# Mirrored spectral pairs, deeper weight prefetch and new filler rates in a fused forward and backward block

## The chip, the cores and the metric

The kernel runs on one core of one Trainium2 chip. The metric is device time in microseconds (us), the median of several executions. "PE" is TensorE, "PEld" its weight load, "DVE" VectorE, "ACT" ScalarE, "POOL" GpSimd, "SP" SyncE.

## The reference

The reference computes one block and all gradients of it. An adaptive layer norm goes into a spectral filter (a two-dimensional real Fourier transform, a complex product with a filter, and back), a second layer norm goes into a bilinear gated layer, and then everything is differentiated.

```python
# x: (1, 2048, 576) bf16; w_r, w_i: (2048, 289); w_gate, w_up: (576, 4608); w_down: (4608, 576)
def _A_ref(x, w_r, w_i):
    X = jnp.fft.rfft2(x.astype(jnp.float32), axes=(-2, -1))
    X = X * (w_r + 1j * w_i)
    return jnp.fft.irfft2(X, s=(S, D), axes=(-2, -1)).astype(jnp.bfloat16)
def _B_ref(x, w_gate, w_up, w_down):
    h = (x @ w_gate) * (x @ w_up)
    return h @ w_down
# sa, ca, ga, sb, cb, gb: six rows of silu(c) @ w_mod
h = layernorm(x) * (1 + ca) + sa
x = x + ga * _A_ref(h, w_r, w_i)
h = layernorm(x) * (1 + cb) + sb
x = x + gb * _B_ref(h, w_gate, w_up, w_down)
# outputs: x and, by jax.vjp with grad_out, the gradients of x, w_r, w_i, w_gate, w_up, w_down, c, w_mod
```

## The kernel before

The transforms are matrix products. The 2048 points are split as 16 times 128, and the spectral part works on eight pairs of the 16 residues k2: (0, 8) and (k, 16 − k). For each pair, `pz` is the transform along D, `px` the one along the 128 points, `cA` the product with the filter, and `pb` the way back. This happens twice: in the head (forward) and in the tail (backward, with the gradient of the filter in `g_w`).

The program has these stages, and the text uses these names for them: the start (loads, transposes, first transforms), the head pairs, the head's way out (`pv`, `py`), the rest of `ghp`, the main loop (the gated layer, about 980 us), t1 (first half of the tail), the tail pairs, t4 (the tail's way out with layer norm gradient), the close (remaining filler) and the end.

TensorE is kept busy by filler: the spectral stages are generators, and at each `yield r` the driver lets r units of independent products run. In the head the filler is `ghp` (the gradient through w_down); in the tail it is `po` (the forward output product, one unit is 18 matmuls).

```python
def pair_x(st, i, kk, gt, fps, ev):                  # 8 matmuls for each kk, 16 for a pair
    C, Sn, nC, nS = (gt[:, kk, v, :] for v in range(4))
    # ... i == 0 cut
    if kk == 0:
        terms = [[(C, 0, 0), (Sn, 0, 1), (Sn, 1, 0), (nC, 1, 1)], [(nS, 0, 0), (C, 0, 1), (C, 1, 0), (Sn, 1, 1)]]
    else:
        terms = [[(C, 0, 0), (Sn, 0, 1), (nS, 1, 0), (C, 1, 1)], [(nS, 0, 0), (C, 0, 1), (nC, 1, 0), (nS, 1, 1)]]
    # ... each c: four matmuls accumulate into px[:, c]; ScalarE evicts px to X (bf16)

def pairs(...):                                       # the order for one pair, `fill` = units of filler
    for i in range(8):
        yield fill
        z(i + 2, 0)
        yield fill
        z(i + 2, 1)
        x(i + 1, 0)
        yield fill
        x(i + 1, 1)                                   # evicts X, then cmul on VectorE makes Ys[i + 1]
        pair_b(i, 0, Ys[i], tbb[i], ut, fps, ev)
        yield fill
        pair_b(i, 1, Ys[i], tbb[i], ut, fps, "a")
        on_b(i, st[i]["X"])                           # tail: g_w, the gradient of the filter

# head:  fill 0.5;  filler ghp, its weights loaded AH blocks ahead
AH = 4
def ghh_units():
    for fb, k in ...:
        if k == 0 and fb + AH < NFB:
            load_wdT(fb + AH)                         # two transposing DMAs
        st = u4w.tile([128, 8, 128], BF, name="ghh_st", bufs=4)
        # ... 10 matmuls into pg (ghp), ScalarE evicts pg to st, DMA writes st to DRAM

# tail pairs: fill 0.35;  t4: 1.55 units at each of 16 steps;  then the close runs what is left
yield from pairs(wk, gsp, T, hT, ut, fps, True, lambda i, X: None, g_w, 0.35, "a")
# g_w: pA, pB are f32 products of the saved spectrum and the gradient; gw = their sum and difference (bf16)
```

## Time and profile before

| | before |
|---|---|
| median of the 4 runs known at the prediction | 1561.51 us (1551.31 to 1568.61) |
| span of the profiled execution | 1566.8 us |
| PE busy | 1502.3 us, 96% |
| DVE busy | 805.6 us, 51% |
| main loop's first matmul | 272.56 us |

The page of the kernel before starts with the busy time of each engine, its share of the span, and its number of instructions.

```profile
PE 1502.3 (96%) x11275; PEld 1035.4 (66%) x11275; DVE 805.6 (51%) x1867; ACT 486.9 (31%) x827; POOL 307.3 (20%) x514
```

TensorE is the bound: a page with 96% there leaves 64 us of idle time in all. The view of waits for PE says where that idle time went. The columns are: the waiting engine, tile and line, what it waited for, the total in us, how many times, and the longest.

```profile
PE gwp L607 <- DMA hh_sf<-hhT: 10.0, 5, 2.8
PE py L329 <- DVE dm L815: 7.2, 2, 6.7
PE ghp L440 <- DMA wdT<-in_B_w_down_dram: 6.7, 1, 6.7
PE po L944 <- DMA wdr<-in_B_w_down_dram: 4.7, 2, 3.8
PE gwp L607 <- DVE so L611: 4.0, 1, 4.0
...
PE ghp L440 <- ACT ghh_st L441: 3.7, 3, 1.6
```

Several of these are single waits of 4 to 7 us, and two of them (wdT and wdr) are late loads of weights, which a program can simply issue earlier.

The table of stretches gives the busy time of each engine in a window. The columns are the window, its length, busy us with the number of instructions in brackets for PE, PEld, DVE, ACT and POOL, the granted TensorE clock as a share of full speed, the busy share of the DMA engines, and GB/s.

```profile
75.00:160.00 85.00, 84.56 (x566) 54.84 (x565) 27.41 (x41) 39.36 (x55) 22.62 (x45) 1.00 0.60 171
258.00:265.40 7.40, 0.75 (x4) 0.14 (x3) 0.00 (x0) 1.01 (x1) 1.06 (x2) 0.92 0.50 125
265.40:272.50 7.10, 7.10 (x20) 2.56 (x20) 0.00 (x0) 1.01 (x1) 0.54 (x1) 0.61 0.29 60
1352.00:1427.00 75.00, 72.52 (x596) 57.73 (x594) 52.93 (x83) 35.26 (x55) 18.92 (x37) 1.00 0.75 241
```

The first and last rows are the two spectral stages: PE is busy nearly all of both, so matmuls removed there are worth their time, if nothing else takes their place. The two rows between are the wait for wdT and what follows it. The second is nearly empty, and in the third the granted clock is 0.61. The timeline of PE around that place (start, duration, engine, line, operation, in brackets the idle time ahead and what ended it) shows the cost:

```profile
249.96 8.79 PE L440 MATMUL ghp<-goT,wdT 128*128 128x512 bf16 x40 [0.62 <-ACT ghh_st L441]
265.40 7.23 PE L440 MATMUL ghp<-goT,wdT 128*128 128x512 bf16 x20 [6.65 <-DMA wdT<-in_B_w_down_dram]
272.56 0.60 PE L656 MATMUL abp<-h2T,wgu 64*128 64x512 bf16 x4
```

Forty matmuls took 8.79 us before the gap, and the next twenty took 7.23 us, where half of 8.79 would be 4.4.

The view by tile counts the matmuls of the spectral part (operation, output and inputs, number; then shortest, median and longest duration in ns, and the first and last start):

```profile
L226 PE MATMUL px<-zt,gt x240: 283/287/288, 75.0 to 1418.4; 128*128 128x290 bf16 x120
...
L243 PE MATMUL pb<-gbt,cA x360: 270/273/283, 85.2 to 1427.1; 128*128 128x256 bf16 x180
```

The 287 ns are the latency of one; pipelined, they follow each other every 0.11 to 0.125 us.

### The profile page before, as it was taken

Reading aid. Unit: us, or ns where it says so; the run is one execution under the profiler, and the core shown is the slowest. Engines: PE = TensorE matmul, PEld = TensorE weight load, DVE = VectorE, ACT = ScalarE, POOL = GpSimd, SP = SyncE. Lnnn points to the kernel's source line nnn. Section 1 sums busy time; section 2 is a strip of 40 time slices with the busy share of each in tenths; the row PEclk is TensorE's granted clock in tenths of the full one; section 3 lists DMA queues with packets and bytes.
Section 4 is the critical chain, followed back from the end, with each engine's and each line's share of the span. In section 5 each row is a group of like instructions: output and inputs, shape, how many; then the busy total and the mean of one; then the engine's idle time right before and its main releaser. Section 6 shows DMA issues by size and latency. Waiting matters only on the chain. (4 is left out here: it accounts for less than half of the span.)

```text
span 1566.8 us, 28323 instructions
## 1 busy us (share of the span) xinstructions
PE 1502.3 (96%) x11275; PEld 1035.4 (66%) x11275; DVE 805.6 (51%) x1867; ACT 486.9 (31%) x827; POOL 307.3 (20%) x514
## 2 busy tenths in 40 slices
PE   7899998999999999999999999999999988999788
PEld 4466553568667767766856866776676666777566
DVE  5533572624633653553462464365356377467664
ACT  4554553230231132123023023112212334444323
POOL 2132343212211211111111121121120121122210
PEclk9999999999999999999999999999999998999899
DMA  9965797957865874895595686587467497667663
GB/s 283 210 185 169 223 250 212 154 116 136 157 118 123 161 160 91 142 169 118 134 142 105 145 159 144 96 157 170 96 150 144 89 323 256 218 193 261 211 227 95
DMA packets 408993, 262.12 MB, mean 167 GB/s; under 512 B 322555, under 2 KB 374012, under 8 KB 408604
## 3 DMA queue, kind: packets, MB, share of 16 engines
q1 hardware_dynamic: 374810, 143.61, 44.8%
q0 software_dynamic: 34048, 116.70, 27.1%
q8 instruction: 88, 1.44, 0.4%
q14 instruction: 45, 0.37, 0.1%
q10 hardware_dynamic: 2, 0.00, 0.0%
HBM read 107.30 MB, written 77.15 MB: 118 GB/s over the span
## 5 line engine op out<-in xcount | busy, mean ns | idle before, releaser
L688 PE MATMUL abp<-wT,ggT 128*128 128x288 bf16 x1152 | 283.0, 286 | 0.0
L689 PE MATMUL abp<-wT,guT 128*128 128x288 bf16 x1152 | 283.0, 286 | 0.0
L662 PE MATMUL abp<-h2T,wgu 128*128 128x512 bf16 x1152 | 261.1, 380 | 0.0
L694 DVE TENSOR_TENSOR acc<-acc,abp 128x288 f32<-128x288 f32 x544 | 240.8, 453 | 20.5 <-PE abp L689 5.3
L668 DVE TENSOR_TENSOR guT<-ghh,gT 128x512 bf16<-128x512 bf16 x144 | 61.3, 425 | 360.1 <-ACT gT L664 355.8
L620 PEld LDWEIGHTS <-h2p 128*128 128x128 bf16 x2304 | 225.7, 98 | 30.4 <-issue 3.4
L621 ACT CAST wo<-gwp 128x256 bf16<-128x256 f32 x144 | 53.5, 372 | 600.4 <-PE gwp L620 567.0
L662 PEld LDWEIGHTS <-wgu 128*128 128x128 bf16 x1152 | 106.8, 98 | 149.5 <-issue 30.5
L440 PE MATMUL ghp<-goT,wdT 128*128 128x512 bf16 x720 | 165.5, 384 | 11.2 <-DMA wdT<-in_B_w_down_dram 6.7
L607 PE MATMUL gwp<-gon,hh_sf 128*128 128x288 bf16 x1152 | 149.4, 291 | 14.0 <-DMA hh_sf<-hhT 10.0
L944 PE MATMUL po<-wdr,hl 128*128 128x288 bf16 x1152 | 153.4, 292 | 4.7 <-DMA wdr<-in_B_w_down_dram 4.7
L607 PEld LDWEIGHTS <-hh_sf 128*128 128x128 bf16 x1152 | 114.0, 99 | 46.3 <-DMA hh_sf<-hhT 11.6
L944 PEld LDWEIGHTS <-hl 128*128 128x128 bf16 x1152 | 114.0, 100 | 38.4 <-issue 7.7
L688 PEld LDWEIGHTS <-ggT 128*128 128x128 bf16 x1152 | 112.7, 98 | 30.2
L689 PEld LDWEIGHTS <-guT 128*128 128x128 bf16 x1152 | 112.7, 98 | 30.0
L620 PE MATMUL gwp<-gu_sf,h2p 128*128 128x256 bf16 x1152 | 130.1, 274 | 2.0 <-ACT wo L621 2.0
L440 PEld LDWEIGHTS <-wdT 128*128 128x128 bf16 x720 | 70.7, 99 | 91.1 <-issue 9.1
L620 PE MATMUL gwp<-gg_sf,h2p 128*128 128x256 bf16 x1152 | 129.3, 273 | 0.0
L612 POOL TENSOR_TENSOR dgb_p<-dgb_p,pr 128x288 f32<-128x288 f32 x72 | 58.0, 805 | 295.4 <-DVE pr L610 290.4
L664 ACT CAST gT<-abp 128x512 bf16<-128x512 f32 x144 | 84.4, 586 | 84.0 <-PE abp L662 84.0
L441 ACT CAST ghh_st<-ghp 128x1024 bf16<-128x1024 f32 x72 | 72.5, 1009 | 94.6 <-PE ghp L440 61.5
L664 ACT CAST uT<-abp 128x512 bf16<-128x512 f32 x144 | 84.4, 586 | 46.1 <-PE abp L662 46.1
(181 smaller groups left out, 1530.9 us busy)
## 6 DMA issues: line engine op xcount, KB each, us to landing
ghhT_d<-ghh_st POOLq DMA_DIRECT2D x72, 256.0 KB, 4.0
ghh<-ghhT_d POOLq DMA_DIRECT2D x36, 512.0 KB, 8.8
hhT_d<-hhT POOLq DMA_DIRECT2D x36, 512.0 KB, 6.4
hl<-hhT_d SPq DMA_DIRECT2D x32, 576.0 KB, 8.3
out_dram<-wo SPq DMA_DIRECT2D x36, 256.0 KB, 2.4
so<-in_B_w_down_dram POOLq DMA_DIRECT2D x36, 144.0 KB, 2.4
out_dram<-so SPq DMA_DIRECT2D x36, 144.0 KB, 1.9
gbt<-tab_GB POOLq DMA_DIRECT2D x16, 320.0 KB, 4.2
```

The costliest lines, as they stand in the source:

```text
L440: nc.tensor.matmul(pg[:, b, :], lhsT=wdT[:, m, :], rhs=goT[:, ts_, m, :], start=(m == 0), stop=(m == 4))
L441: nc.scalar.copy(st[:], pg[:].rearrange("f b (t p) -> f (b t) p", p=128))
L607: nc.tensor.matmul(pw[:, 0:288], lhsT=hh_sf[:, j, t, :], rhs=gon[:, t, h * 288:(h + 1) * 288], start=(t == 0), stop=(t == NT - 1))
L612: nc.gpsimd.tensor_tensor(out=dgb_p[:, hs_], in0=dgb_p[:, hs_], in1=pr[:], op=ADD)
L620: nc.tensor.matmul(pw[:], lhsT=h2p[:, t, m * 128:(m + 1) * 128], rhs=sf[:, :, t, :], start=(t == 0), stop=(t == NT - 1))
L662: nc.tensor.matmul(pts[k][i][:], lhsT=wgu[:, 4 * i + m, cs], rhs=h2T[:, ts_, m, :], start=False, stop=(m == 3))
L664: nc.scalar.copy(dst[:], pts[k][i][:])
L668: nc.vector.tensor_tensor(out=guT[:, ts_, :], in0=ghh[:, ts_, :], in1=gu[0][:], op=MUL)
L688: nc.tensor.matmul(pu[:, 0:288], lhsT=ggTs[j][:, t, :], rhs=wT[:, 0, j, hs_], start=(j == 0), stop=False)
L689: nc.tensor.matmul(pu[:, 0:288], lhsT=guTs[j][:, t, :], rhs=wT[:, 1, j, hs_], start=False, stop=(j == G - 1))
L694: nc.vector.tensor_tensor(out=dst, in0=dst, in1=pu[:, 0:288], op=ADD)
L944: nc.tensor.matmul(po[:, 0:288], lhsT=hl[:, fb, j * 128:(j + 1) * 128], rhs=wdr[fb][0][:, fb - wdr[fb][1], hs_], start=(fb == 0), stop=(fb ...
```

## The change

The intent is to use a symmetry. The rows of residue 16 − k are those of residue k in mirrored order, so one cosine and one sine product serve both members of a pair. VectorE then forms the sum and the difference of the even part E and the odd part O. This halves `px` and `pb` for seven of eight pairs, in head and tail. The second member comes out with its rows k1 reversed, so the filter is first copied in DRAM in mirrored order (`wrev_d`), and the gradient is written mirrored (`grev_d`) and copied back. Around it, other things move:

- wdT is loaded nine blocks ahead instead of four, and `ghh_st` has five buffers instead of four.
- In the tail the leftover rows of the last weight gradient go first, the first `po` products are split in another order, and one load of wdr is issued one step later.
- The row `rc` is loaded ahead.
- The filler rates go from 0.35 to 0.5 in the tail pairs and from 1.55 to 1.4 in t4.
- Some pools have other depths, and one memset goes from POOL to VectorE.

The core of the diff, with cuts marked:

```diff
-            for v, m in enumerate((C, Sn, -C, -Sn)):
+            for v, m in enumerate((C, Sn, -Sn)):
                 G[:, i, kk, v, :] = m
...
         elif kk == 0:
-            terms = [[(C, 0, 0), (Sn, 0, 1), (Sn, 1, 0), (nC, 1, 1)], [(nS, 0, 0), (C, 0, 1), (C, 1, 0), (Sn, 1, 1)]]
+            terms = [[(C, 0, c), (Sn, 1, c)] for c in (0, 1)]
         else:
-            terms = [[(C, 0, 0), (Sn, 0, 1), (nS, 1, 0), (C, 1, 1)], [(nS, 0, 0), (C, 0, 1), (nC, 1, 0), (nS, 1, 1)]]
+            terms = [[(C, 1, c), (nS, 0, c)] for c in (1, 0)]
...
-        evac(X[:, kk, :, :], px[:, :, 0:FQ], ev)
+        if i > 0:
+            st[i][kk] = wk.tile([128, 2, FQ], FP32, name="EO", tag="w")
+            evac(st[i][kk][:], px[:, :, 0:FQ], ev)
...
+            nc.vector.tensor_tensor(out=X4[:, 2:0:-1, :], in0=E[:], in1=O[:], op=ADD)
+            nc.vector.tensor_tensor(out=X4[:, 0:4:3, :], in0=E[:], in1=O[:], op=SUB)
... (pair_b: two terms instead of four for each half)
@@ cmul
-        return A
+        if not mix:
+            return A
+        nc.vector.tensor_tensor(out=B[:, 0, :, :], in0=A[:, 0, :, :], in1=A[:, 1, :, :], op=ADD)
+        nc.vector.tensor_tensor(out=B[:, 1, :, :], in0=A[:, 0, :, :], in1=A[:, 1, :, :], op=SUB)
+        return B
@@ head
-        AH = 4
+        AH = 9
-            wdTs[fb] = u4w.tile([128, 5, 128], BF, name="wdT")
+            wdTs[fb] = u4w.tile([128, 5, 128], BF, name="wdT", bufs=10)
-        load_wdT(3)
+        for fb in range(3, 9):
+            load_wdT(fb)
-                st = u4w.tile([128, 8, 128], BF, name="ghh_st", bufs=4)
+                st = u4w.tile([128, 8, 128], BF, name="ghh_st", bufs=5)
+                    for k, v in enumerate((wr_v, wi_v)):
+                        nc.gpsimd.dma_start(wrev_d[k], mirrored(v))
@@ tail
-        last_grads = grads(NFB - G, hh_sf, gg_sf, gu_sf)
+        last_grads = grads(NFB - G, hh_sf, gg_sf, gu_sf, True)      # left_rows first
-            nc.gpsimd.memset(h[:, :, D:D + 2], 0.0)
+            nc.vector.memset(h[:, :, D:D + 2], 0.0)
-                yield from pairs(wk, gsp, T, hT, ut, fps, True, lambda i, X: None, g_w, 0.35, "a")
+                yield from pairs(wk, gsp, T, hT, ut, fps, True, lambda i, X: None, g_w, 0.5, "a")
+            load_rc(0)
-                        yield 1.55
+                        yield 1.4
-                if k in (3, 7, 12):
+                if k in (3, 8, 12):
-                    for h in range(2):
+                    for h, k in ((0, 0), (1, 0), (0, 1), (1, 1)) if t == 0 else ((0, 0), (0, 1), (1, 0), (1, 1)):
... (mirrored writes of the gradient, table loads, pool depths: cut)
```

## The prediction

> **What bounds the kernel now.** TensorE. The page gives PE 1502 of 1567 us (96%), DVE 51%, ACT 31%. By the table of stretches PE is also busy 24–25 of every 25 us in both spectral stages that the change rewrites: 75–160 us (head pairs) and 1352–1428 us (tail pairs). PE time removed there should mostly be span. The Trainium skill, "TensorE: Matmul & The Clock Gate" (HAM oscillation), warns against PE gaps above about 3.4 us; this trace agrees: after the 6.65 us gap at 258.7 us the granted clock is 0.61 and 20 matmuls of 512 take 7.2 us instead of 4.4.
>
> **Removed.** The waits by tile give 240 matmuls for px and 360 for pb. With even/odd sums formed on VectorE, each of 7 pairs in each of two stages needs 8 instead of 16 px and 12 instead of 24 pb matmuls: 112 and 168 fewer. The timeline shows 8 px in 1.00 us and 24 pb in 2.62 us, so 0.125 and 0.109 us each: 14.0 + 18.3 = 32 us of PE, half in the head, half in the tail.
>
> **Added.** Per pair, two f32 combinations (0.756 us each for 580 elements, as the gw group) and two bf16 mixes (0.455 us): 2.4 us of DVE. Head pairs: period 10.55 us now, 8.3 after by PE; DVE about 6. Fits, but px groups are now 0.5 us, shorter than their 0.64 us ACT evictions in two PSUM buffers behind a 1.01 us ghh_st eviction: I estimate 0.7 us of new PE stall per pair. Tail pairs: DVE rises from about 6.5 to 9 us per pair, PE falls to 8.2 (with more filler), so VectorE becomes co-critical; perhaps 6 us is lost. The mirrored DRAM copy (1 MB at about 45 us, where the DMA share is already 1.0) risks a few us.
>
> **Moved.** Nine-deep wdT prefetch should remove the 6.65 us wait for wdT plus the 2.8 us of slow clock behind it. A fifth ghh_st buffer: part of 3.1 us. left_rows moved first and the split order at t = 0 take the 4.7 us wait of po on wdr. Filler rates 0.5 and 1.4 leave 10 instead of 13 po units to cover the closing chain, which exposes about 5 us. The t4 stage loses 16 us of PE to DMA and DVE waits now and will not give its whole saving.
>
> **Sum.** Head: 16 − 5 stalls + 9.4 + 2 = −22 us. Tail: 16 − 6 − 4 (t4) − 5 (end) + 4.7 + 1 = −7 to −12. In all −29 to −34: **1529 us**, 8 in 10 between 1511 and 1546. Chances: faster by over 2% 0.56, within 2% 0.42, slower 0.02.
>
> **What would show each step right.** px 128 and pb 192 matmuls; PE busy down about 30 us; head pairs' period near 9 us with short PE waits on ACT evictions of pz/px; the main loop's first matmul at about 248–252 us instead of 272.6; no wait of ghp on wdT over 2 us and no clock dip before the main loop; no wait of po on wdr; DVE over 85% busy in the tail pairs, with PE waits there on DVE.
>
> **What would make it wrong.** VectorE order: if the ut cast queues behind the new mixes, pb's PSUM is held and head pairs keep their 10.5 us. If mirrored copies starve the head, the 25–75 us stretch grows. If tail DVE backlog stretches t4, the tail gains nothing and the result is about 1540. If DVE keeps up and t4 loses its stalls, about 1512.

## The result and the profile after

| | before | after |
|---|---|---|
| median | 1555.57 us (1546.23 to 1568.61, 16 runs) | 1509.48 us (1506.74 to 1515.5, 11 runs) |
| PE busy in the profiled execution | 1502.3 us | 1460.6 us |
| DVE busy | 805.6 us | 834.9 us |
| main loop's first matmul | 272.56 us | 251.32 us |

The ratio is 0.9704, with a 95% interval from 0.9677 to 0.9731: about 3% faster. A ratio here and below is the mean time of one kernel's fast runs over that of the other's of the same rounds, so not quite the ratio of the medians that are quoted. The predicted 1529 us was too high, and the time lies just below the range that began at 1511. (The record lists a twelfth execution of after, of 1504.36 us, which its summary of 11 runs leaves out.)

The page of the kernel after, the engines:

```profile
PE 1460.6 (97%) x10995; PEld 1005.0 (67%) x10995; DVE 834.9 (55%) x1925; ACT 485.8 (32%) x827; POOL 311.0 (21%) x516
```

The waits of PE, after:

```profile
PE pb L255 <- DVE cB L334: 7.1, 3, 3.5
PE po L985 <- ACT mo L988: 5.2, 1, 5.2
PE pgc L1010 <- DVE gcf L1008: 4.9, 1, 4.9
PE px L227 <- ACT zt L158: 3.9, 12, 0.4
```

None of the five leading waits of before is among them. In their place stand the new ones: `pb` waits for the mixed product `cB` of VectorE, `px` for the evictions of ScalarE, and the last small transpose `pgc` is now exposed at the end.

The timeline of PE, after, at the place where wdT had been late:

```profile
239.79 11.60 PE L464 MATMUL ghp<-goT,wdT 128*128 128x512 bf16 x53
251.32 0.60 PE L692 MATMUL abp<-h2T,wgu 64*128 64x512 bf16 x4
```

Fifty-three matmuls in 11.60 us is 0.219 us for each, with no gap. By tile, after:

```profile
L227 PE MATMUL px<-zt,gt x128: 283/285/288, 71.0 to 1373.9; 128*128 128x290 bf16 x128
...
L255 PE MATMUL pb<-gbt,cB x168: 269/272/421, 92.5 to 1389.6; 128*128 128x256 bf16 x168
L255 PE MATMUL pb<-gbt,cA x24: 269/272/273, 80.8 to 1327.5; 128*128 128x256 bf16 x24
```

That is 128 `px` and 168 + 24 = 192 `pb`, as the prediction had them.

To see where the time came from, both kernels were profiled again (the runs b_again and a_again below), because the first profile of before had caught the slowest of its 16 runs. The boundaries of the stages are first and last matmuls of `pz`, `pv`, `abp` and `po` in the traces, and each stage is the difference of two such times.

| stage (us) | before, first profile | before, second | after, second | second after − second before |
|---|---|---|---|---|
| start | 72.6 | 71.5 | 68.5 | −3.0 |
| head pairs | 89.6 | 89.7 | 77.9 | −11.8 |
| head's way out | 64.3 | 64.3 | 64.2 | −0.1 |
| rest of ghp | 46.1 | 46.4 | 35.7 | −10.7 |
| main loop | 993.8 | 984.2 | 981.4 | −2.8 |
| t1 | 86.8 | 85.6 | 80.6 | −5.0 |
| tail pairs | 74.4 | 74.0 | 77.2 | +3.2 |
| t4 | 92.8 | 88.7 | 77.1 | −11.6 |
| close | 42.0 | 42.0 | 34.1 | −7.9 |
| end | 4.4 | 4.4 | 10.6 | +6.2 |
| span | 1566.8 | 1550.8 | 1507.3 | −43.5 |

The last four stages belong together, because the filler moves between them: they take 209.1 us before and 199.0 us after, so the tail behind t1 gained 10.1 us.

### The profile page after: what moved, and what is told of

Same layout as the page of the kernel before. It is cut to its first block, busy times and chain, and to the rows that moved or that the text cites. A ratio compares the mean times of both kernels' runs of the same rounds, so it can differ in the third digit from the quotient of the medians.

```text
span 1511.1 us, 27920 instructions
## 1 busy us (share of the span) xinstructions
PE 1460.6 (97%) x10995; PEld 1005.0 (67%) x10995; DVE 834.9 (55%) x1925; ACT 485.8 (32%) x827; POOL 311.0 (21%) x516
## 5 line engine op out<-in xcount | busy, mean ns | idle before, releaser
L646 PE MATMUL gwp<-gon,hh_sf 128*128 128x288 bf16 x1152 | 144.1, 286 | 0.0
L700 ACT CAST uT<-abp 128x512 bf16<-128x512 f32 x144 | 84.4, 586 | 46.1 <-PE abp L698 46.1
L465 ACT CAST ghh_st<-ghp 128x1024 bf16<-128x1024 f32 x72 | 72.6, 1010 | 82.2 <-PE ghp L464 62.3
```

The lines of the kernel that those rows point to most:

```text
L465: nc.scalar.copy(st[:], pg[:].rearrange("f b (t p) -> f (b t) p", p=128))
L646: nc.tensor.matmul(pw[:, 0:288], lhsT=hh_sf[:, j, t, :], rhs=gon[:, t, h * 288:(h + 1) * 288], start=(t == 0), stop=(t == NT - 1))
L700: nc.scalar.copy(dst[:], pts[k][i][:])
```

## The experiments

The kernels of one session ran on the same chip and share the runs of the kernel before; five sessions were run. Sessions 2 and 3 ran on one chip, with seven runs of before in common. A trace is one execution; the medians are of several. All kernels gave correct results.

| run | median us (range) | ratio to before | 95% interval |
|---|---|---|---|
| session 1, before | 1560.13 (1553.45 to 1566.79) | | |
| b_again | 1552.65 (one run) | | |
| b_wdt | 1545.01 (1542.82 to 1546.87) | 0.9897 | 0.9856 to 0.9938 |
| a_nowdt | 1528.53 (1523.9 to 1532.08) | 0.9794 | 0.9755 to 0.9834 |
| b_spec | 1534.71 (1531.46 to 1541.59) | 0.9841 | 0.9798 to 0.9885 |
| session 2, before | 1562.22 (1552.62 to 1569.86) | | |
| a_again | 1508.16 (1506.87 to 1516.13) | 0.9662 | 0.9611 to 0.9712 |
| a_fill | 1513.77 (1510.43 to 1518.33) | 0.9686 | 0.9628 to 0.9743 |
| a_norc | 1508.36 (1504.55 to 1514.55) | 0.9656 | 0.9605 to 0.9707 |
| a_last | 1511.71 (1508.49 to 1511.75) | 0.9669 | 0.9624 to 0.9713 |
| session 3, before | 1563.07 (1552.62 to 1569.86) | | |
| a_t4slow | 1510.79 (1509.46 to 1511.18) | 0.9666 | 0.9613 to 0.9718 |
| a_bfw | 1510.07 (1508.31 to 1511.01) | 0.9662 | 0.9617 to 0.9706 |
| a_t4fast | 1508.54 (1507.86 to 1518.01) | 0.9667 | 0.9615 to 0.9719 |
| a_latew | 1508.14 (1507.23 to 1509.65) | 0.9654 | 0.9602 to 0.9706 |
| session 4, before | 1560.72 (1552.92 to 1563.09) | | |
| a_gap | 1524.04 (1519.56 to 1524.61) | 0.9768 | 0.9736 to 0.9801 |
| a_nowdt2 | 1520.56 (1519.4 to 1523.17) | 0.9756 | 0.9719 to 0.9793 |
| a_fillbf | 1503.55 (1501.97 to 1506.92) | 0.9646 | 0.9614 to 0.9678 |
| a_both | 1509.31 (1507.18 to 1511.86) | 0.9681 | 0.9648 to 0.9713 |
| session 5, before | 1557.83 (1552.85 to 1562.3) | | |
| a_fillbf2 | 1505.68 (1501.15 to 1511.95) | 0.9669 | 0.9645 to 0.9693 |
| a_again2 | 1510.68 (1506.7 to 1516.46) | 0.9695 | 0.9673 to 0.9717 |

### The two kernels again: b_again, a_again, a_again2

No edit; each is the kernel before or after, word for word.

> The kernel before, unchanged, for a second profile. Theory 1: the 10 us that TensorE waited for hh_sf transposes in the main loop of the first profile (which was the slowest of 16 runs) are partly chance; this profile shows the first main-loop matmul at 271 to 274 us again, but under 6 us of hh_sf waits, and a span of 1548 to 1560. Rival: the waits belong to the program's order, and 9 to 11 us come back at the same places.

> The kernel after, unchanged, for a second profile. Theory: the main loop's waits on hh_sf transposes are rarer in the kernel after; main loop (first to last of its matmul groups) 979 to 983 us and under 3 us of hh_sf waits, against 984 and 994 us with 3.9 and 10.0 us in the two profiles of before. Rival: the first profile of after was lucky, and this one shows 4 us or more of such waits.

> The kernel after verbatim, beside the bf16 version on the same chip: 1505 to 1511 us, no waits on hh_sf in the first 60 us of the main loop, head pairs 77.9 us, tail pairs with t4, closing stage and end 199 us.

The span of b_again was 1550.8 us, 16.0 us less than the first profile of the same kernel. The stage table above shows where: 9.6 us in the main loop, where the first profile had waited 10.0 us for hh_sf, and 4.1 us in t4. So waits on hh_sf and in t4 come and go between executions of before; the pair b_again and a_again compares a quick execution of before with an ordinary one of after.

a_again took 1507.3 us and a_again2 1514.7 us. Nearly all of that difference is in the head pairs: 77.9 against 84.5 us (82.7 in the first profile of after). The expectation of 77.9 us for a_again2 was a miss. The waits of VectorE in a_again2 between 69 and 110 us name what had happened:

```profile
DVE cB L329 <- DMA wn<-wrev_d: 4.0, 1, 4.0
DVE cA L328 <- DMA wn<-wrev_d: 3.3, 1, 3.3
```

and its table of stretches shows the consequence for PE:

```profile
90.00:95.00 5.00, 0.51 (x5) 0.18 (x2) 2.23 (x5) 0.88 (x2) 1.04 (x3) 0.98 0.91 208
95.00:100.00 5.00, 5.00 (x22) 2.56 (x22) 4.54 (x8) 0.16 (x1) 0.69 (x2) 0.67 1.06 313
```

The mirrored filter came too late, PE stood still for 4.5 us, and the clock fell to 0.67 afterwards. In the first profile of after VectorE waited 4.2 and 1.2 us on `wrev_d` there. In a_again it did not at all. No other wait of PE between 60 and 150 us differs by more than 0.3 us, though why the copy is late in some executions was not tested. In the seventeen profiles with mirrored copies the head pairs took 77.8 or 77.9 us in thirteen, and 78.8 to 84.5 us in the other four (b_spec, a_fillbf, the first profile of after, a_again2). So the mirrored copies did hurt the head now and then, as the prediction feared, but through a late operand in the pairs and not by stretching the start: the start stage was 68 to 69 us in these profiles, against 71.5 and 72.6 before.

### The spectral part alone: b_spec

The edit keeps the mirrored spectral part, its buffers and its copies, and puts everything else back.

```diff
--- after
+++ b_spec
-        AH = 9
+        AH = 4
-  ... bufs=10 (wdT), bufs=5 (ghh_st), six early loads of wdT
+  ... bufs=6 (wdT), bufs=4 (ghh_st), one early load of wdT
-                yield from pairs(..., g_w, 0.5, "a")        # tail pairs
+                yield from pairs(..., g_w, 0.35, "a")
-                        yield 1.4                           # t4
+                        yield 1.55
   ... rc loaded at its use, left_rows last, old order of po, wdr loads at 3, 7, 12, memset on POOL
```

> The spectral part of the change alone (halved px and pb, mirrored copies, smaller tables, one more buffer); prefetch, ghh_st, order of the last gradients, rc loads and filler rates as before. Theory: head pairs give 7 to 11 us and the tail 7 to 12 us, the rest nothing: ratio 0.985 to 0.991. Rival: the tail gives nearly all 16 us because VectorE keeps up, and the stage after it loses its stalls too: 0.980 or less.

The time was 1534.71 us, ratio 0.9841. In the head the part did its work: the head pairs took 78.8 us, 10.9 less than in b_again. In the tail these profiles show almost no gain. These are the stretches of the tail pairs, of t4, and of close with end, first for b_again:

```profile
1341.70:1415.70 74.00, 72.69 (x594) 57.78 (x594) 53.50 (x84) 34.75 (x55) 18.99 (x37) 1.00 0.75 239
1415.70:1504.40 88.70, 78.41 (x631) 57.81 (x632) 60.27 (x151) 35.13 (x56) 19.47 (x34) 0.94 0.67 214
1504.40:1550.80 46.40, 41.68 (x336) 31.51 (x333) 24.07 (x61) 16.70 (x29) 2.89 (x5) 0.98 0.35 118
```

then for b_spec:

```profile
1331.60:1402.70 71.10, 60.69 (x455) 45.04 (x456) 63.26 (x103) 34.43 (x55) 18.32 (x37) 0.96 0.70 213
1402.70:1493.00 90.30, 81.51 (x632) 59.09 (x633) 64.05 (x160) 34.97 (x56) 20.18 (x35) 0.92 0.66 214
1493.00:1539.80 46.80, 41.66 (x336) 31.51 (x333) 24.06 (x61) 16.72 (x29) 3.65 (x6) 1.00 0.45 146
```

PE's work in the tail pairs fell by 12.0 us (72.69 to 60.69), the stage by 2.9 us only, and the three rows together by 0.9 us (209.1 to 208.2). VectorE rose to 63.26 us of 71.10. Much of what the change took from TensorE came back as a wait on VectorE in the tail pairs, as the waits of PE in b_spec show there:

```profile
PE pb L255 <- DVE cB L334: 7.3, 3, 4.1
```

Two cautions belong to this. The tail of before differs between executions: it took 213.6 us in the first profile, 209.1 us in b_again and 211.3 us in b_wdt, which has the tail of before; so the spectral part alone gained 1 to 5 us there, not surely 0.9. And the two profiles are unlike: b_again was 7.5 us quicker than the median of before in its session, and b_spec's profile was the slowest of its four. By the traces the spectral part gained 11.0 us, by the medians 25 us (by the interval 18 to 32; the ratio is just below the expected 0.985 to 0.991). Where the other 14 us lie these traces do not show. a_fill, below, is the better comparison for the tail.

### The filler rates: a_fill, a_t4slow, a_t4fast

```diff
--- after
+++ a_fill
-  ... g_w, 0.5, "a")
+  ... g_w, 0.35, "a")
-                        yield 1.4
+                        yield 1.55
```

a_t4slow changes only the 1.4 to 1.55, and a_t4fast changes it to 1.2.

> The kernel after with the old filler rates (0.35 in the tail pairs, 1.55 in the stage after). Theory: tail pairs stay VectorE-bound and lose little time (74 to 76 us instead of 77.5) although five po units (11 us of PE) leave them; the stage after and the close take those units: t4 +6 us, close +6 us, end -6 us, so 4 to 8 us slower than after, ratio to before 0.973 to 0.976. Rival: the filler rates are also what removed the stage's 12 us of waits and slow clock: 12 us or more slower, 0.978 and up.

> The kernel after with the old filler rate of 1.55 in the stage after the tail pairs, and the new 0.5 in the pairs. Two and a half po units (5.3 us) move from the close into that stage. Theory: above about 1.4 the fillers delay the chain ring load, n1, py, u and bring back waits: the stage takes 84 to 87 us instead of 77. Rival: the stage just takes the units it is given, 82 to 83 us, and its shortening from 89 us came from something else.

> The kernel after with filler rate 1.2 in the stage after the tail pairs: three more po units are left for the close. Theory: the closing chain is covered again (end 4 to 5 us instead of 10.6, close 41 us instead of 34) and the stage, then bound by VectorE, takes 72 to 75 us instead of 77: together 2 to 5 us faster than after. Rival: the stage cannot shorten below 77, and nothing is gained.

a_fill was 5.6 us slower than a_again in the same session (1513.77 against 1508.16; the intervals of the ratios overlap). The tail's three rows in a_again:

```profile
1308.30:1385.50 77.20, 72.53 (x562) 55.90 (x563) 66.90 (x108) 35.46 (x57) 21.05 (x41) 0.96 0.69 216
1385.50:1462.60 77.10, 71.26 (x579) 52.17 (x578) 61.60 (x157) 33.65 (x54) 17.38 (x30) 0.98 0.70 228
1462.60:1507.30 44.70, 35.08 (x282) 26.31 (x279) 23.36 (x59) 18.06 (x29) 3.65 (x6) 0.94 0.49 158
```

and in a_fill:

```profile
1306.60:1379.00 72.40, 61.06 (x454) 45.25 (x454) 63.39 (x103) 34.52 (x55) 18.83 (x38) 0.95 0.67 209
1379.00:1465.20 86.20, 80.17 (x632) 58.56 (x633) 64.08 (x160) 34.82 (x56) 19.55 (x34) 0.95 0.69 224
1465.20:1513.70 48.50, 43.32 (x336) 32.21 (x333) 24.14 (x61) 17.05 (x29) 3.64 (x6) 0.94 0.43 141
```

At the old rates PE is idle 72.40 − 61.06 = 11.3 us of the tail pairs, at the new ones 77.20 − 72.53 = 4.7 us. The stage becomes 4.8 us longer with the higher rate, but 11.5 us more of PE's work is done in it, and t4 and the close become shorter by more. Summed, 207.1 us become 199.0 us. The other profiles of after have 198.9 and 200.6 us.

Only 2.4 us of these 8.1 us are idle time of PE (22.5 us in a_fill, 20.1 us in a_again). The other 5.7 us are busy time: nearly the same number of matmuls, 1422 and 1423 records, was busy for 184.6 us in a_fill and for 178.9 us in a_again. The granted clock agrees in direction: in the tail pairs and t4 it was 0.95 and 0.95 in a_fill, 0.96 and 0.92 in b_spec, and 0.96 and 0.98 in a_again. Which wait led to which dip was not traced.

The expectation of a_fill was right in the size of the loss (4 to 8 us), but not in the ratio (0.973 to 0.976) nor in the stages: the tail pairs took less than its 74 to 76 us, and t4 and the close each grew by over 9 us instead of 6.

The rate of t4 has little room. This is t4 in a_t4slow and then in a_t4fast:

```profile
1383.30:1468.40 85.10, 76.93 (x615) 56.30 (x614) 63.23 (x159) 33.91 (x55) 17.92 (x31) 0.96 0.71 233
1384.80:1460.00 75.20, 63.96 (x526) 46.20 (x523) 60.87 (x155) 32.94 (x53) 17.34 (x30) 1.00 0.73 235
```

With 1.55 (a_t4slow) t4 took 85.1 us and the tail 203.9 us; with 1.2 (a_t4fast) t4 took 75.2 us and the tail 200.2 us. Going from 1.4 to 1.55 put 2.4 more units into t4 and cost 8.0 us there, 3.3 us a unit; going down to 1.2 took 3.2 units out and gained 1.9 us, 0.6 us a unit. A unit is 18 matmuls, about 2.2 us of PE at 0.12 us each. At 1.2 PE was idle 75.20 − 63.96 = 11.2 us of t4 (by the table of stretches), at 1.4 it was 5.8 us, and at 1.55 it was 8.2 us, with a single wait of 3.5 us on VectorE among them that in the profile at 1.4 is 0.6 us. So at 1.2 PE lacks work in t4, and 1.4 fills it; whether 1.55 is worse for more than that one wait, one profile does not tell. The medians of the three (1510.79, 1508.16, 1508.54) show no clear difference. The gain of 2 to 5 us expected of a_t4fast did not come: the end was covered again (4.7 us) and t4 shrank, but the close grew by 7.9 us. Taken one by one, the rate of the pairs is worth 3.2 us of the tail (207.1 to 203.9) and the rate of t4 4.9 us (203.9 to 199.0), each by single profiles.

### VectorE in the tail pairs: a_bfw, a_fillbf, a_fillbf2

The edit stores the f32 products pA and pB of `g_w` in bf16, which rounds the gradient of the filter slightly more. The Trainium skill says in "VectorE: DVE Perf Modes", section "What auto-detection actually checks", that the engine takes the double rate for an operation on two tensors if every tensor is 16 bits wide with a step of one. This trace agrees in direction: with one f32 tensor on one side, the product of 1160 elements took 1.355 us and the sum of 580 elements 0.755 us; with bf16 on both sides they took 0.757 and 0.456 us, which is 1.79 and 1.66 times as fast.

```diff
--- after (a_bfw), a_fill (a_fillbf and a_fillbf2)
-  late["pA"], late["pB"] = (view(a2[:, 6144 + ...], [128, 2, 2, FQ]) for k in range(2))
+  late["pA"], late["pB"] = (view(a2[:, 6144 + ...].bitcast(BF), [128, 2, 2, FQ]) for k in range(2))
```

> The kernel after with the products pA and pB of the w gradients in bf16 instead of f32 (outputs rounded a little more). It takes about 1.8 us of VectorE time from each tail pair. Theory: VectorE bounds the tail pairs: the wait of pb on cB goes, the stage falls from 77 to 72 to 74 us, ratio to before 0.963 to 0.966. Rival: ACT and the two PSUM buffers bound it: 76 us or more, no change in time.

> The kernel after with the old rates of filler (0.35 and 1.55) and the f32 products of the gradient in bf16 (output rounded slightly more). Theory (at the low rate of filler VectorE paces the tail pairs): the stage falls from 72.4 us to 64 to 68 us, VectorE busy below 52 us, the wait of pb on cB shrinks below 3 us, time 1507 to 1511 us. Rival (the chain of ScalarE evictions and two PSUM buffers paces it): stage 71 to 73 us, time 1512 to 1515 us.

> The same kernel again: the old rates of filler and the bf16 products. Theory (its lead over after in the last session, 1503.6 against 1508 to 1509, was noise, as its four tail stages together took 198.3 us against 199.0 us): within 0.2% of after in the same session. Rival (it is 4 to 5 us faster): ratio lower than that of after by 0.003 and intervals apart.

At the new filler rates the edit did nothing for the time (1510.07 us in its session). VectorE's work in the tail pairs fell from 66.90 us to 56.06 us, and the stage only from 77.2 to 75.8 us: PE was busy 70.27 us of it. VectorE is not the bound there, and the expected fall to 72 to 74 us was missed.

At the old filler rates the same edit did much. The tail's three rows in a_fillbf:

```profile
1306.80:1372.70 65.90, 59.22 (x455) 44.56 (x456) 52.94 (x108) 34.75 (x55) 18.80 (x37) 0.97 0.76 235
1372.70:1456.40 83.70, 79.85 (x631) 58.55 (x632) 60.95 (x155) 33.85 (x54) 18.59 (x32) 0.94 0.63 201
1456.40:1505.10 48.70, 43.34 (x336) 32.28 (x333) 24.16 (x61) 18.12 (x31) 4.72 (x8) 0.96 0.56 185
```

The tail pairs fell from 72.40 us to 65.90 us with nothing but VectorE's work taken away (10.5 us of it), which is what was expected of a stage that VectorE paces, though VectorE's 52.94 us are a little more than the 52 expected and the wait of `pb` for `cB` shrank only from 7.3 to 4.9 us, not below 3. The rival, that evictions and PSUM buffers pace it at 71 to 73 us, is out; and since the same evictions fit into 65.9 us here, they do not set the 75.8 us of a_bfw either. So VectorE paces the tail pairs at the old rates and TensorE at the new ones. The tail's total is 198.3 us, against 199.0 in a_again and 198.5 in a_bfw: in these profiles more filler and faster VectorE are two ways to the same gain, and doing both adds nothing.

a_fillbf had the shortest median of its session, 1503.55 us, below the 1507 to 1511 us expected. Repeated with five rounds it gave 1505.68 us against 1510.68 us of after in the same session, with ratios 0.9669 and 0.9695. The intervals overlap, so this version is perhaps 0.3% faster than after; it is not shown. The profile of a_fillbf2 (1499.4 us) had a tail of 193.7 us, 4.6 us less than the same kernel in a_fillbf, and that of a_again2 a late mirrored filter in the head.

### The prefetch of wdT: b_wdt, a_nowdt, a_nowdt2, a_gap

b_wdt puts the deeper prefetch alone into before; a_nowdt and a_nowdt2 (the same kernel twice) take it alone out of after. a_gap keeps it, and makes a gap of the same length at the same place by other means: nine ScalarE copies and one dummy matmul that waits for them.

```diff
--- before
+++ b_wdt            (a_nowdt: the reverse, from after)
-        AH = 4
+        AH = 9
-            wdTs[fb] = u4w.tile([128, 5, 128], BF, name="wdT")
+            wdTs[fb] = u4w.tile([128, 5, 128], BF, name="wdT", bufs=10)
-        load_wdT(3)
+        for fb in range(3, 9):
+            load_wdT(fb)
--- after
+++ a_gap
+                if fb == NFB - 1 and k == 0:
+                    for _ in range(9):
+                        nc.scalar.copy(late_t[:], last[0][:, 0:6, :].rearrange("f t p -> f (t p)"))
+                    nc.tensor.matmul(pg[:, 0, 0:128], lhsT=late_t[:, 0:128], rhs=late_t[:, 0:128], start=True, stop=True)
+                last[0] = st
```

> The kernel before with the nine-deep wdT prefetch alone. Theory: only the gap before the main loop goes (6.7 us of waiting and 2.8 us of slow clock): ratio 0.993 to 0.995, first main-loop matmul at 262 to 264 us, main loop otherwise as before. Rival A: the main loop's hh_sf waits depend on what the queue still holds at the hand-over and go too: ratio 0.987 or less. Rival B: the early transposes crowd the saturated start and give half back: 0.997.

> The kernel after with the old four-deep wdT prefetch. Theory: the gap before the main loop comes back, 8 to 11 us: ratio to before 0.976 to 0.979 (after has 0.970), a wait of ghp on wdT over 5 us and a granted clock under 0.9 just before the main loop. Rival: the smaller DMA load of the new spectral part already frees the queue, and the ratio stays at 0.970 to 0.973.

> The kernel after with nine-deep prefetch kept, but the TensorE held up for about 8 us ahead of the last block of ghp products by nine ScalarE copies and one small dummy matmul. So the gap and the slow clock behind it come back, at the place and size of the late wdT, without the late wdT load. Theory (the gap itself costs more than its length, because of what comes after it): time near that of four-deep prefetch, 1524 to 1530 us, and waits of PE on hh_sf of 3 us or more in the first 60 us of the main loop. Rival (the late loads themselves slow the first transposes of the main loop): only the gap and the slow clock are added, 10 us, so 1517 to 1520 us, and no waits on hh_sf in the first 60 us.

> The kernel after with four-deep prefetch, verbatim again, to stand beside the run with the made gap on the same chip: 1525 to 1531 us, a wait of 7 to 8 us on wdT, waits on hh_sf of about 3 us in the first 60 us of the main loop.

In the traces the prefetch is worth its gap and its slow clock. The rest of `ghp` takes 46.4 us in b_again and 37.3 in b_wdt, 45.6 in a_nowdt, 45.8 in a_nowdt2 and 35.7 in a_again: 9 to 10 us, where the prediction had 6.65 + 2.8 = 9.4.

In the times it was worth more. b_wdt has the ratio 0.9897, which is 16 us of 1560, with an interval from 10 to 22 us. a_nowdt and a_nowdt2 have 0.9794 and 0.9756, after itself 0.9704, 0.9662 and 0.9695; the difference of the means is 0.0088, or 14 us. The 0.9897 of b_wdt lies between its two expectations (0.993 to 0.995, and 0.987 or less).

After session 1 there seemed to be a reason for the surplus. In the first 60 us of the main loop PE had waited for hh_sf, for 5.2 us in before, 3.3 in b_again, 4.1 in b_spec and 2.9 in a_nowdt, all with four-deep prefetch, and not at all in any profile with nine-deep prefetch (two by then, fourteen in the end, a_gap not counted). a_gap was to tell whether the gap or the late load caused this. These are the rows of the PE timeline of a_gap:

```profile
250.50 0.29 PE L464 MATMUL ghp<-late_t 128*128 128x128 bf16 x1 [8.91 <-ACT late_t L463]
250.58 6.97 PE L469 MATMUL ghp<-goT,wdT 128*128 128x512 bf16 x20
```

and of a_nowdt2:

```profile
251.04 5.99 PE L463 MATMUL ghp<-goT,wdT 128*128 128x512 bf16 x20 [8.07 <-DMA wdT<-in_B_w_down_dram]
```

The gap without the late load cost as much as the gap with it: 1524.04 and 1520.56 us. So the gap is what costs, and the load is not. But neither profile had the waits on hh_sf: none in a_gap and 0.4 us in a_nowdt2. Both expectations were missed in part, the 1525 to 1531 us of a_nowdt2 and the waits of a_gap. What the surplus of 4 to 6 us over the 10 us in the traces consists of stays open. It is not clear of the noise: the interval of b_wdt reaches down to 10 us, and a_nowdt2 was 11.3 us above a_both, the nearest to after in its session. The waits at the start of the main loop are seen in four of five profiles with four-deep prefetch and in none with nine-deep, the one with the made gap included, so they seem to go with the late load and not with the gap; but nothing shows how, and in a_nowdt2 they were nearly absent.

The Trainium skill, "TensorE: Matmul & The Clock Gate", section "What's actually happening", says that the array's clock halves after an idle window of about 3.4 us and returns after about as long a busy one. The three gaps here, all longer than that, agree that a slow stretch follows and ends: after 6.65, 8.07 and 8.91 us of idle the same twenty matmuls took 7.23, 5.99 and 6.97 us, where 4.4 us is the undisturbed time; the slow clock thus cost 1.6 to 2.8 us, not in proportion to the gap. If the clock was halved, that is an estimate of 3.2 to 5.7 us of slow clock, so two of the three were longer than the page's figure.

### The late wdr and the order of the last step: a_last

```diff
--- after
+++ a_last
-        last_grads = grads(NFB - G, hh_sf, gg_sf, gu_sf, True)
+        last_grads = grads(NFB - G, hh_sf, gg_sf, gu_sf)
-                if k in (3, 8, 12):
+                if k in (3, 7, 12):
   ... and the old order of the first po products
```

> The kernel after with left_rows at the end of the last gradients, the wdr loads at the old steps, and po of t = 0 in the old order. Theory: the wait of po on wdr comes back, 4 to 8 us with its slow clock: ratio to before 0.973 to 0.976, the stage between main loop and tail pairs 85 to 89 us instead of 81. Rival: the wait moves elsewhere and nothing changes, under 2 us.

The wait came back, as the waits of PE in a_last show:

```profile
PE po L985 <- DMA wdr<-in_B_w_down_dram: 6.8, 2, 3.9
```

t1 grew from 80.6 to 83.6 us, and the time from 1508.16 to 1511.71 us. The direction and the size of about 3 us agree with the prediction's 4.7 us, if not all of it; the intervals of the ratios overlap, and the expected 4 to 8 us, 85 to 89 us and ratio of 0.973 to 0.976 were all missed on the low side. a_again has a new wait of 5.0 us in t1 in exchange, of `po` on the eviction `mo`.

### The row rc loaded ahead: a_norc

```diff
--- after
+++ a_norc
-            load_rc(0)
   ... and rc loaded where it is used, as in before
```

> The kernel after with the rc rows loaded where they are used, as before. Theory: the 6.5 us wait of py on dm behind a late ring load in the stage after the tail pairs was tied to the queue order, and the early rc load removes it: 5 to 9 us slower than after, ratio to before 0.974 to 0.977. Rival: rc was never what dm waited for (it waited behind ring loads in VectorE's queue): no change, 0.970 to 0.972, and no py wait over 2 us.

The median was 1508.36 us against 1508.16, and t4 took 77.3 us against 77.1: the early load of `rc` is worth nothing here. The wait of `py` on `dm` (6.4 us in one piece in b_again) went away all the same; 0.8 us is left of it. At the old filler rates half of it stayed, wherever `rc` was loaded: 3.2 us in b_spec (at its use) and 3.3 us in a_fill (ahead). The timeline of VectorE in before shows why loading `rc` was not the point:

```profile
1462.75 0.76 DVE L900 TENSOR_TENSOR t4ring<-t4ring 128x1152 bf16<-128x1152 bf16 x1 [2.12 <-DMA t4ring<-y_d]
1463.42 0.75 DVE L815 TENSOR_TENSOR dm<-fpb,rc 128x576 f32<-128x576 f32 x1
```

`dm` followed directly on an operation that had waited 2.12 us for a DMA of the ring, on the same engine. The wait named `dm`, but what was late was `y_d`.

### The weights of the next step issued later: a_latew, a_both

```diff
--- after
+++ a_latew
-            if g0 + G < NFB:
-                wgu = load_w(g0 + G)
-            else:
+            if g0 + G >= NFB:
   ...
             if g0 + G < NFB:
+                wgu = load_w(g0 + G)
                 wT = load_wT(g0 + G)
```

a_both is a_latew with the t4 rate 1.2.

> The kernel after with the w_gate and w_up loads of the next main-loop step issued after the accumulation block instead of before it, so that they do not share the DMA engines with the hh_sf, gg_sf and gu_sf transposes. Theory: the scattered waits on hh_sf are DMA contention just there: no hh_sf waits, main loop 979 to 980 us, run to run spread smaller, 1 to 3 us faster in the mean. Rival: the contention is with the gradient stores or the transposes alone: waits as before, or the loads now come late themselves and the main loop grows.

> The kernel after with the next step's weights loaded behind the acc block and t4 rate 1.2. Theory (the two single differences were noise): 1507 to 1511 us, within 0.2% of after. Rival (each is worth about 1 us): 1504 to 1506.5 us.

a_latew was meant for the waits on hh_sf in the main loop. It had none and a main loop of 979.5 us, but so had a_fill, a_t4slow and a_t4fast without the edit, and the median was 1508.14 us against 1508.16. a_both gave 1509.31 us, and had 2.6 us of waits on hh_sf and a main loop of 982.6 us with the edit. Nothing is gained: the single small leads were noise.

## Why the prediction was right or wrong

The direction was right and most mechanisms were; the size was not. Predicted was a gain of 29 to 34 us; the median of before minus that of after is 46 us, and the two traces compared above differ by 43.5 us. By stages of these traces, the head gave 25.6 us for the predicted 22, t1 5.0 for 4.7, the tail behind t1 10.1 for 2, and the main loop 2.8 for nothing. PE's busy time fell by 41.7 us between the first profiles and 35.7 us between the second ones, for the predicted 30 to 32.

**The head pairs: right.** Predicted −11 us (16 us of matmuls less 5 us of new stalls), measured −11.8 us and, for the part alone, −10.9 us. The short waits of `px` on `zt` came as foreseen (12 times, at most 0.4 us).

**The prefetch: mechanism right, somewhat small.** The gap and the slow clock are 9 to 10 us in the traces for the predicted 9.4, and the dip of the clock is gone. The times say 14 to 16 us with wide intervals. a_gap shows that the gap itself is the cost.

**The fifth ghh_st buffer and the start: not shown.** Predicted 2 us; the 3.7 us of waits on `ghh_st` are gone from the profile of after, and the start became 3.0 us shorter. No run took this edit alone, and the buffer is not the whole reason: with five buffers and the old prefetch the waits were 3.9 us in a_nowdt and 0.4 us in a_nowdt2, with four buffers and the new prefetch 1.2 us in b_wdt. The start was 73.1 us in a_nowdt and 69.5 us in b_wdt.

**wdr: the wait went, but the number fits in part by luck.** Predicted 4.7 us; t1 became 5.0 us shorter, of which a_last gives 3 us to this edit. And a part of that is another wait: `gwp` on `so`, 4.2 us in b_again and 0.9 in a_again. It stays at 4.0 us in b_spec, where the memset was on POOL, and at 0.9 us in a_last, where it was on VectorE. That suggests the memset, which the prediction did not count; no run isolates it.

**The tail pairs, t4 and the end: the step that failed.** The prediction put "16 − 6 − 4 − 5 + 1" there, a gain of about 2 us apart from wdr. Measured were 10.1 us (209.1 to 199.0). Two of its terms were there. In the tail pairs of b_spec PE had 12.0 us less work and the stage became only 2.9 us shorter, so more than the 6 us was lost to VectorE. The exposed end cost 6.2 us for the predicted 5.

What failed is the term for t4, which "will not give its whole saving": a loss of 4 us was predicted, and t4 became 11.6 us shorter with 52 fewer matmuls, about 6.2 us of work at 0.12 us each. a_t4slow, which changes this one rate, shows the same: from 1.55 to 1.4, 36 matmuls or about 4.3 us leave t4 and it becomes 8.0 us shorter. With it failed the adding up of the terms as losses that stay. The new rates bring the exposed end, but they also take a part of the other losses away, because a unit that covers idle time in the tail pairs is missing from t4 and the close.

By the rows above, PE's idle time in the tail was 16.3 us in b_again, 24.3 us in b_spec, 22.5 us in a_fill, and 20.1 us in a_again, and its busy time 192.8, 183.9, 184.6 and 178.9 us. From b_again to a_again the busy time fell by 13.9 us and the idle time rose by 3.8 us, where the prediction had let it rise by 6 + 4 + 5 − 1 = 14. From a_fill to a_again most of the gain is that the matmuls were busy for a shorter time, 5.7 us, which the prediction had no term for.

The prediction had named this outcome among the ways to be wrong: "If DVE keeps up and t4 loses its stalls, about 1512." The time came close to that; VectorE did not quite keep up, but t4 lost about half of its idle time (10.3 to 5.8 us).

**VectorE at over 85% with PE waiting on it: seen, but not the bound.** VectorE was busy 66.9 of 77.2 us (87%), and `pb` waited on it. Yet a_bfw, which takes 10.8 us off VectorE, gained nothing. At the rates of after, TensorE paces the stage; at the old rates (a_fillbf) VectorE does.

**The base.** The prediction started from 1561.51 us, the median of four runs; over all sixteen it was 1555.57. In that comparison 6 us of the missing 20 are base. In other sessions before had medians from 1557.83 to 1563.07, so this share depends on the session.

**The main loop: not in the prediction.** It became 2.8 us shorter between the second profiles, and 12.4 us against the first profile of before. Nothing in the change touches it. Both kernels wait for hh_sf there, at varying places; with nine-deep prefetch too (6.5 us in b_wdt, 5.3 us in a_norc, whose loop took 988.6 us). Four-deep prefetch goes together with such waits at its start, but in a_nowdt2 they were 0.4 us. This stays open.

**Chance in the head.** The mirrored copies cost nothing that shows in most profiles and about 5 to 7 us of the head pairs in two of the three profiles of after. The prediction named the copies as a risk and looked for it in the wrong stretch.

## What to carry to other kernels

When independent work fills the gaps of the busiest engine, do not add up the losses of the stages one by one: add up that engine's work over all stages that share the filler, and estimate its remaining idle time and what it runs slower there, because a filler unit that makes one stage longer makes another shorter. A saving on the busiest engine can vanish into the engine that received the work (here VectorE), and it comes back if the stage gets more filler or the second engine less work, but not twice. And a named wait on an engine may belong to whatever stood in its queue ahead, so an edit for a wait should be tested alone.

## What the Trainium skill lacked or had wrong

- "TensorE: Matmul & The Clock Gate": the page does not say how much a single gap well beyond its window costs ahead of dense matmuls, or how that varies. Here gaps of 6.65, 8.07 and 8.91 us ahead of the same twenty 512-wide matmuls cost 2.8, 1.6 and 2.6 us by the slow clock: the penalty did not grow with the gap.
- No page says how much a load that reads freshly mirrored DRAM copies varies between executions: waits on such a load in the head, all by VectorE, were 0 us in one profile of the kernel after and 5.4 and 7.3 us in the two others.
